# The MLP's down product as full 128x128 matmuls instead of 64x64 quarters, in a fused RWKV-7 and MLP kernel

## Chip, cores and metric

The kernel runs on one core of a Trainium2 chip. The metric is the device time of one execution in microseconds (us). Three runs of the kernel before took 823.68, 815.56 and 818.89 us; their median is 818.89. Besides, one execution was taken with the hardware profiler; every row of a profile is from that one execution.

TensorE (PE in the views) multiplies: a matmul holds a stationary operand, which a weight load (PEld) brings into the array, and streams the columns of the moving operand through it. VectorE is DVE, ScalarE ACT, GpSimd POOL, and SyncE SP; SP issues the DMA transfers here.

## The reference

An RWKV-7 recurrence over 768 steps for 4 batches and 8 heads of 40 channels, and then an MLP of 320 to 2048 to 320 features on its 3072 output rows, all in fp32:

```python
for t in range(S):                                   # attention, S = 768
    y[:, :, t] = np.einsum('bhd,bhde->bhe', rt, state)
    Sa = np.einsum('bhde,bhe->bhd', state, at)
    state_decay = state * wt[:, :, None, :] - np.einsum('bhd,bhe->bhde', Sa, bt)
    state = state_decay + np.einsum('bhd,bhe->bhde', vt, kt)
...
h = x @ w_in                                         # x: (3072, 320), w_in: (320, 2048)
g = h * (1.0 / (1.0 + np.exp(-1.702 * h)))
return (g @ w_out).astype(np.float32)                # w_out: (2048, 320)
```

The change concerns the last line, `g @ w_out`.

## The kernel before

**Work.** The sequence is cut into 12 chunks of 64 steps. A unit is one chunk of two batches, so there are 24 units, two for each chunk. For a unit the kernel prepares decays (`decay`, `prep`), solves the recurrence inside the chunk in a chain of small products (`solve`: a score N, then six `level` steps in two halves b, then the outputs y and the carried state z), and sends the result x through a DRAM tile into `xT`. After the second unit of a chunk the MLP of that chunk follows (`mlp`, L834), on 256 tokens: 4 batches of 64 steps.

**Products.** Every product in the file goes through the helper `mm` (L270), so all matmuls carry line 271. All of them are in 64x64 quarters of the array: `HALF` (L241) names the two halves of the 128 partitions and `QUARTERS` (L243) the order of the four combinations (half that is read, half that is written). In the down product (L851 to L862) a stationary tile is 64 rows of g (features) by 64 tokens, and the moving one is 64 rows of `w_out_sb` by 320 columns:

```python
for r, b in QUARTERS:
    o = p * 128 + b * 64
    mm(po[HALF[b], r, :DM], g[HALF[r], f % 2, o:o + 64], w_out_sb[HALF[r], f * DM:(f + 1) * DM], f == 0)
```

The two feature halves r of a block f of 128 features accumulate in different PSUM banks, bank r of a pair, and b names the token half on the partitions. So after 16 blocks f the result is the sum of two banks. Each fp32 product is executed as two passes, each with its own weight load: 1,536 calls of `mm` are 3,072 matmuls and 3,072 loads in the trace.

For one chunk, `up` (L837) makes the hidden layer in four tiles q of four blocks f; `gelu` (L846) brings each of them from PSUM into a buffer g (four buffers, `g=4` in L252). `down(p)` (L851) is called for each token half p (two batches). Its `part(m)` does two blocks f, 8 calls of `mm`, and there are eight parts for each p: 192 in all. One pair of banks serves one p. `store` (L867) then copies bank 0 into the buffer `ob` (ACT or DVE, L871), adds bank 1 to it on DVE (L873), and issues two output DMAs (L870). `ob` has one buffer.

**Order.** Nothing here is in program order. Each step is added to a planner (`Plan`, L59) as a task with a rank, the engines that may do it, an estimated cost on each, the data it reads and writes, and its PSUM pair (four pairs of two banks, `psum`, L265). `Plan.order` (L97) places tasks on the engines one after the other: of the tasks that are ready, the lowest rank goes first. Solving has ranks below 300, the MLP 10000 and more, so that ups and downs fill what the solver's chain leaves of TensorE. `paced` (L204) tries four release times for the MLP and keeps the plan that it finds shortest. For TensorE the planner also counts instructions (`instr`), since it assumes that they are fetched in blocks of 256 (`BLOCK`, `FETCH`, L65, and `fetched`, L133), and prefers tasks with fewer of them when it is ahead of the fetch. `pe` (L277) gives a TensorE task its cost: two passes of columns / 1.2 + 3 ns for each quartet, and 16 instructions. The instructions are then emitted in the order found; each engine works through its own in that order and waits on semaphores.

Of the kernel before, what the change touches and what calls it, by code (L numbers as in the profile page):

```python
# [49 lines left out]

class Task:
    def __init__(self, rank, engines, fn, pair, most, size):
        self.instr, self.sbuf = engines.pop("instr", 0), engines.pop("sbuf", False)
        self.rank, self.fn, self.pair, self.most, self.size = rank, fn, pair, most, size
        self.engines = engines
        self.after, self.then, self.release = set(), [], 0.0


class Plan:  # L59
# [5 lines left out]
    BLOCK, FETCH, BESIDE, AHEAD = 256, 3550.0, 0.4, 300.0  # L65
    DELAY = {"PE": 300.0, "DVE": 60.0, "ACT": 60.0, "POOL": 150.0, "SP": 800.0}

    LATENCY, RATE, SPREAD = 1200.0, 400.0, 1.3

    def __init__(self, slots, pairs):  # L70
        self.slots, self.pairs = slots, pairs
# [25 lines left out]
    def order(self):  # L97
# [10 lines left out]
        able, now, wire, out, many = [], 0.0, 0.0, [], set()  # L108
# [8 lines left out]
                return clear > len({o.pair[0] for o in able if o.most is not None and o.pair not in held and not any(k[0] == o.pair[0] for k in many)})  # L117
            return clear > 0 and sum(k[0] == t.pair[0] for k in many) < t.most

        issued, begun, shared = 0, 0.0, 0.0  # L120

        def fetch(at):
            took = self.FETCH
# [9 lines left out]
        def fetched(t, start):  # L133

            at, left, ns, block = start, t.instr, t.engines["PE"] / t.instr, begun
            room = self.BLOCK - issued % self.BLOCK
            while left >= room:
                at += room * ns
                left -= room
                at = block = max(at, block + fetch(block))  # L140
                room = self.BLOCK
            return at + left * ns, block
# [5 lines left out]
        while coming or able:  # L148
            while coming and coming[0][0] <= now:
                able.append(self.tasks[heapq.heappop(coming)[1]])  # L150
            able.sort(key=lambda t: (t.rank, t.n))
            took = None
            for e in free:
                if free[e] <= now:
                    took = next((t for t in able if e in t.engines and fits(t) and unread(t, e) <= now), None)
                    if took and e == "PE" and ahead(took) > self.AHEAD:

                        took = next((t for t in able if e in t.engines and fits(t) and ahead(t) < min(self.AHEAD, ahead(took))), took)
                    if took:
                        break  # L160
            if not took:
                later = [x for x in (*free.values(), *pairs, *(unread(t, e) for t in able for e in t.engines)) if now < x < float("inf")]
                now = min(later + ([coming[0][0]] if coming else []))
                continue
            t = took
            able.remove(t)
            t.engine = e
            end = now + t.engines[e]
            if e == "PE":
                end, begun = fetched(t, now)  # L170
                issued += t.instr
            if e == "POOL" or e == "DVE" and t.sbuf:

                shared = max(now, shared) + t.engines[e]
                end = max(end, shared)
            free[e] = end
            if e == "SP":
                wire = max(wire, end + self.LATENCY)
                running.append((wire, wire + self.SPREAD * t.size / self.RATE))
                end = wire = running[-1][1]  # L180
            if t.pair is not None:
                if e != "PE":
                    last.setdefault(t.pair, {})[e] = end
                if t.pair not in held:
                    held[t.pair] = next(i for i, p in enumerate(pairs) if p <= now)
                    pairs[held[t.pair]] = float("inf")
                    if t.most is not None:
                        many.add(t.pair)
                t.bank = held[t.pair]
                users[t.pair] -= 1  # L190
                if not users[t.pair]:
                    many.discard(t.pair)
                    pairs[t.bank] = end + self.DELAY[e]
            for o in t.then:
                o.ready = max(o.ready, end + (0.0 if o.engines.keys() == {e} else self.DELAY[e]))
                o.left -= 1
                if not o.left:
                    heapq.heappush(coming, (max(o.ready, o.release), o.n))
            t.start = now
            out.append(t)  # L200
# [24 lines left out]
def rwkv7_gelu_quick(ctx: ExitStack, tc: tile.TileContext, time_d, v_d, w_d, wc_d, ak_d, b_d, rv_d, w_in, w_out, out):  # L225
    nc = tc.nc
    H, D, S = 8, 40, out.shape[0] // 4
    DM = H * D
# [3 lines left out]
    PIECE = w_in.shape[2]  # L232
    NF = w_in.shape[0] * PIECE // DM
    NM = NF // 2
    NK = DM // 64
    NQ = NM // 2
# [4 lines left out]
    HALF = [slice(0, 64), slice(64, 128)]  # L241
    BITS = (0, 1)
    QUARTERS = [(0, 0), (1, 1), (0, 1), (1, 0)]  # L243
# [5 lines left out]
    banks = ctx.enter_context(tc.tile_pool(name="banks", bufs=1, space=bass.MemoryType.PSUM))  # L249

    plan = Plan(dict(logw=3, wc=3, G=1, wch=3, wz=2, time=2, ak=2, b=2, rv=2, FT=3, GT=1, kh=2, bh=2, bz=2,
                     A=1, Av=1, RV=2, W=2, W0=2, W1=2, E=2, E0=2, E1=2, edge=1, zraw=2, zT=1, saT=1, M=2, y=1, x=1, xT=3, g=4, ob=1), 4)  # L252
    tiles, psums, drams = {}, {}, {}

    def single(name, shape):
# [9 lines left out]
    def psum(t, name):  # L265
        if t.pair not in psums:
            psums[t.pair] = banks.tile([128, 2, 512], FP32, tag=f"pair{t.bank}", name=name)
        return psums[t.pair]

    def mm(o, lhsT, rhs, start):  # L270
        nc.tensor.matmul(o, lhsT, rhs, start=start, stop=True, skip_group_check=True)  # L271
# [5 lines left out]
    def pe(*sets):  # L277

        return {"PE": sum(n * 2 * max(58.0, cols / 1.2 + 3) for n, cols in sets), "instr": sum(16 * n for n, _ in sets)}

    def dve(n):
        return {"DVE": 170.0 + 1.03 * n}
# [4 lines left out]
    def any2(n):  # L287
        return {**act(n), **dve(n)}

    def copy(e):  # L290
        return nc.scalar.copy if e == "ACT" else nc.vector.tensor_copy
# [33 lines left out]
    edge = single("edge", [128, 2, 2, 2, 168])  # L325
# [508 lines left out]
    def mlp(c):  # L834
        R = 10000 + 100 * c

        def up(q, m, k):  # L837
            def go(t):
                ph, x = psum(t, "ps_up"), xT_of(c)[:, :, k]
                for r, h in QUARTERS:  # L840
                    mm(ph[HALF[h], r, m * 256:(m + 1) * 256], w_in_sb[HALF[r], 2 * q + m, k, h * 64:(h + 1) * 64], x[HALF[r]],
                       m == 0 and k == 0)
            plan.add(R + q, pe((1, 256)), go, reads=[("xs", (c, p)) for p in BITS] + [("weight", q)],
                     uses=[("xT", c)], room=[("g", c * NQ + q)], pair=("up", c * NQ + q), most=1)

        def gelu(q):  # L846
            plan.add(-45, act(1024), lambda t: nc.scalar.activation(  # L847
                g_of(c * NQ + q).rearrange("p m r n -> p r m n"), psum(t, "").rearrange("p r (m n) -> p r m n", m=2),
                ACT.Gelu_apprx_sigmoid), writes=[("g", c * NQ + q)], pair=("up", c * NQ + q))

        def down(p):  # L851
            serial = 2 * c + p

            def part(m):
                def go(t):
                    po, g = psum(t, "ps_down"), g_of(c * NQ + m // 2)[:, m % 2]
                    for f in (2 * m, 2 * m + 1):
                        for r, b in QUARTERS:
                            o = p * 128 + b * 64
                            mm(po[HALF[b], r, :DM], g[HALF[r], f % 2, o:o + 64], w_out_sb[HALF[r], f * DM:(f + 1) * DM], f == 0)  # L860
                parts = range(2 * m * DM // PIECE, (2 * (m + 1) * DM - 1) // PIECE + 1)
                plan.add(R + 10 * (p + 1) + m, pe((2, 320)), go, reads=[("g", c * NQ + m // 2)] + [("weight", NQ + n) for n in parts],  # L862
                         pair=("down", serial), most=1)
            for m in range(NM):
                part(m)

            def store(t):  # L867
                for b in BITS:
                    o = (2 * p + b) * S + c * C
                    nc.sync.dma_start(out[o:o + C, :], ob_of(serial)[HALF[b]])  # L870
            plan.add(-45, any2(320), lambda t: copy(t.engine)(ob_of(serial), psum(t, "")[:, 0, :DM]),  # L871
                     writes=[("ob", serial)], pair=("down", serial))
            plan.add(-45, dve(320), lambda t: nc.vector.tensor_add(ob_of(serial), ob_of(serial), psum(t, "")[:, 1, :DM]),  # L873
                     reads=[("ob", serial)], writes=[("out", serial)], pair=("down", serial))
            plan.add(-100, {"SP": 700.0}, store, reads=[("ob", serial), ("out", serial)], size=128 * DM * 4)

        for q in range(NQ):
            for m in BITS:
                for k in range(NK):
                    up(q, m, k)  # L880
            gelu(q)
        for p in BITS:
            down(p)

    for i in range(3):
        load_w(i)
# [105 lines left out]
```

## Time and profile before

| | |
|---|---|
| runs | 815.56, 818.89, 823.68 us |
| span of the profiled execution, first to last instruction | 816.7 us |
| mean granted TensorE clock | 0.994 of full |
| up product, matmuls | 3,840 of 64x256, 378 ns each |
| down product, weight loads | 3,072 of 64x64, 133 ns each |
| levels, matmuls with E | 5,888, 230 ns each on average over three shapes |
| DVE, final addition L873 | 24 of 128x320, 482 ns each |
| ACT or DVE, copy out of PSUM L871 | 19 on ACT (427 ns), 5 on DVE (492 ns) |
| ACT, gelu L847 | 48 of 128x1024, 1,026 ns each |
| ACT, copies of level results L726 | waited 176.7 us in 132 waits for the levels |
| output DMAs | 48 of 80 KB |

The page lists no separate time of the profiled execution beside its span; the span lies between the times of the runs. A matmul's length in the trace runs from its first read to a modelled end and so overlaps the next ones: quarters run beside each other, and lengths of single records don't add up to time. What a run of matmuls takes is read from start to start. "x16" behind a group is its number of records; in brackets stands how long the engine had been idle before, and what released it. "issue" is an idle time for which the profile shows no cause. The weight load has a row of its own (PEld).

### The profile page before, as it was taken

How to read it: one execution, taken by the hardware profiler on the slowest of the kernel's cores; microseconds unless marked ns; L12 is line 12 of the kernel's file. 1: busy time of each engine (PE TensorE's matmuls, PEld its weight loads, DVE VectorE, ACT ScalarE, POOL GpSimd, SP SyncE). 2: the span in 40 equal slices, each digit the busy share in tenths (PEclk: the TensorE clock that was granted, in tenths of full speed). 3: DMA queues.
4: the chain of work that ended last, by engine and by line, in shares of the span. 5: the costliest groups of instructions: out<-in, count | busy, mean ns of one | idle time of the engine just before them, and what ended most of it. 6: DMA issues, size and time to landing. Idle time of an engine off the chain costs nothing.

```text
span 816.7 us, 51357 instructions
## 1 busy us (share of the span) xinstructions
PE 749.6 (92%) x24192; PEld 636.1 (78%) x24192; DVE 477.7 (58%) x764; ACT 352.3 (43%) x603; POOL 153.3 (19%) x209
## 2 busy tenths in 40 slices
PE   4567887999999999999999989999999999999997
PEld 3556766787798888788888888887787887899785
DVE  7489778755755755756755654745556545455200
ACT  4376874444344253245254344355346345243210
POOL 4024052012202302302302302302103213200000
PEclk9899999999999999999999999999999999999999
DMA  9834452223403502412412512412403213110200
GB/s 348 329 110 146 136 194 72 70 69 89 134 17 91 152 20 86 133 45 82 138 45 68 152 44 74 141 46 72 142 15 98 71 50 92 40 33 4 60 10 18
DMA packets 32731, 76.31 MB, mean 93 GB/s; under 512 B 5096, under 2 KB 14312, under 8 KB 31496
## 3 DMA queue, kind: packets, MB, share of 16 engines
q1 hardware_dynamic: 32520, 73.03, 28.7%
q8 instruction: 190, 3.11, 1.6%
q14 instruction: 21, 0.17, 0.1%
HBM read 65.14 MB, written 7.86 MB: 89 GB/s over the span
## 4 chain that ended last, share of the span: by engine, by line
PE 79%; ACT 7%; DVE 6%; issue 4%; DMA 3%; SPq 1%; POOL 0%; ACTq 0%; DVEq 0%; POOLq 0%
PE ps_down L271 24%; PE ps_up L271 22%; PE ps_level L271 17%; PE ps_y L271 4%; PE ps_N L271 2%; ACT W L726 2%; PE ps_saT L271 1%; PE ps_Av L271 1%; PE ps_M L271 1%; PE ps_NT L271 1%; PE ps_A L271 1%; PE ps_RV L271 1%; PE ps_rz L271 1%; ACT L847 1%; PE ps_zT L271 1%
## 5 line engine op out<-in xcount | busy, mean ns | idle before, releaser
L271 PE MATMUL ps_up<-xT,w_sb 64*64 64x256 f32 x3840 | 274.5, 378 | 7.6 <-issue 4.5
L271 PE MATMUL ps_down<-w_sb,g 64*64 64x320 f32 x3072 | 243.8, 431 | 2.9 <-DVE w_sb L406 1.6
L726 ACT COPY W<-ps_level 128x672 f32<-128x672 f32 (+1 forms) x164 | 102.4, 626 | 184.2 <-PE ps_level L271 176.7
L271 PEld LDWEIGHTS ps_up<-xT,w_sb 64*64 64x64 f32 x3840 | 159.9, 134 | 27.3 <-issue 7.2
L271 PEld LDWEIGHTS ps_level<-W,E 64*64 64x64 f32 x5888 | 153.0, 134 | 27.9 <-issue 4.5
L271 PEld LDWEIGHTS ps_down<-w_sb,g 64*64 64x64 f32 x3072 | 130.9, 133 | 43.8 <-DVE w_sb L406 2.0
L271 PE MATMUL ps_level<-W,E 64*64 64x64 f32 (+2 forms) x5888 | 152.2, 230 | 7.8 <-issue 2.5
L721 DVE TENSOR_TENSOR E<-twice,ps_level 128x512 f32<-128x512 f32 x120 | 81.8, 686 | 87.8 <-ACT W L726 75.6
L538 POOL TENSOR_TENSOR kh<-time,G 128x320 f32<-128x320 f32 x23 | 20.8, 906 | 414.5 <-issue 289.3
L271 PE MATMUL ps_level<-W 64*64 64x64 f32 (+2 forms) x2560 | 69.4, 239 | 22.1 <-issue 10.3
L271 PEld LDWEIGHTS ps_level<-W 64*64 64x64 f32 x2560 | 66.2, 138 | 29.5 <-issue 15.0
L847 ACT ACTIVATE g<-ps_up 128x1024 f32<-128x1024 f32 x48 | 49.2, 1026 | 42.6 <-PE ps_up L271 42.2
L812 POOL TENSOR_TENSOR x<-y,FT 128x128 f32<-128x128 f32 x88 | 56.1, 667 | 0.7 <-DVE y L802 0.4
L705 DVE TENSOR_TENSOR W<-edge,ps_level 128x672 f32<-128x672 f32 x40 | 33.9, 850 | 12.2 <-PE ps_level L271 11.1
L530 POOL TENSOR_TENSOR ak<-ak,FT 128x512 f32<-128x512 f32 x20 | 27.9, 1394 | 64.1 <-DMA ak<-in_ak 55.8
L873 DVE TENSOR_TENSOR ob<-ob,ps_down 128x320 f32<-128x320 f32 x24 | 11.6, 482 | 48.0 <-ACT ob L871 45.7
L271 PE MATMUL ps_y<-RV,kh 64*64 64x104 f32 x768 | 37.1, 251 | 1.3 <-issue 1.3
L271 PE MATMUL ps_y<-M,bh 64*64 64x104 f32 x768 | 37.5, 250 | 0.5 <-issue 0.4
L726 DVE COPY W<-ps_level 128x672 f32<-128x672 f32 (+1 forms) x36 | 26.4, 733 | 14.2 <-PE ps_level L271 14.1
L271 PEld LDWEIGHTS ps_y<-RV,kh 64*64 64x64 f32 x768 | 29.0, 133 | 4.6 <-issue 2.9
L767 DVE TENSOR_TENSOR M<-ps_M,upper 128x512 f32<-128x512 f32 x24 | 16.6, 690 | 26.5 <-PE ps_M L271 26.4
L716 DVE TENSOR_TENSOR E<-twice,ps_level 128x256 f32<-128x256 f32 x40 | 16.8, 420 | 26.1 <-ACT W L726 16.9
(114 smaller groups left out, 986.0 us busy)
## 6 DMA issues: line engine op xcount, KB each, us to landing
time<-in_time SPq DMA_DIRECT2D x24, 480.0 KB
xT<-x_dram SPq DMA_DIRECT2D x48, 160.0 KB
ak<-in_ak SPq DMA_DIRECT2D x44, 160.0 KB
rv<-in_rv SPq DMA_DIRECT2D x44, 160.0 KB
wc<-in_wc SPq DMA_DIRECT2D x24, 264.0 KB
extra<-in_w_out SPq DMA_DIRECT2D x4, 1280.0 KB
logw<-in_w SPq DMA_DIRECT2D x24, 160.0 KB
RV<-in_v SPq DMA_DIRECT2D x24, 160.0 KB
```

The source lines that it names most:

```text
L271: nc.tensor.matmul(o, lhsT, rhs, start=start, stop=True, skip_group_check=True)
L530: plan.add(R, {"DVE": 690.0, "POOL": 1270.0, "sbuf": True}, lambda t: of(t.engine).tensor_mul(ahT(), ahT(), FT_of(i)), reads=T("ak", "FT") ...
L538: plan.add(R + 4, {"POOL": 870.0, "DVE": 490.0, "sbuf": True}, lambda t, n=n, dst=dst: of(t.engine).tensor_mul(dst(i)[:, :, :D], by_head(t ...
L705: plan.add(key, dve(672), lambda t: nc.vector.tensor_sub(W_of(s + 2)[:, :, b], edge[:, :, b], item(t)[:, :, :, :168]), reads=T("edge"), wr ...
L716: plan.add(key, dve(256), lambda t: nc.vector.tensor_tensor(E_of(es + 2)[:, :, b, :, 64:], wide(ident if early else twice).to_broadcast([1 ...
L721: plan.add(key, dve(512), lambda t: nc.vector.tensor_sub(E_of(es + 2)[:, :, b].rearrange("p h j (n t) -> p h (j n) t", n=2), wide(twice).t ...
L726: plan.add(key, any2(4 * (168 - lo)), lambda t: copy(t.engine)(W_of(s + 2)[:, :, b, :, lo:], item(t)[:, :, :, lo:168]), writes=keeps, pair ...
L767: plan.add(R + 4, dve(512), lambda t: nc.vector.tensor_tensor(M_of(i)[:, :, :64].rearrange("p (e j) t -> p e j t", e=2), psum(t, "")[:, :, ...
L812: of(t.engine).tensor_mul(x[:, b ^ u, b], y_of()[:, at], FT_of(i)[:, at])
L847: plan.add(-45, act(1024), lambda t: nc.scalar.activation(g_of(c * NQ + q).rearrange("p m r n -> p r m n"), psum(t, "").rearrange("p r (m ...
L873: plan.add(-45, dve(320), lambda t: nc.vector.tensor_add(ob_of(serial), ob_of(serial), psum(t, "")[:, 1, :DM]), reads=[("ob", serial)], wr ...
```

## The change

A down task now multiplies with the whole array. The stationary tile is 128 features by 128 tokens, the moving one 128 rows of `w_out_sb` by 320 columns, and one matmul does what a quartet did. The two token halves p of a chunk are done in the same task, each in a bank of its own of one PSUM pair. There are 8 tasks for a chunk, each of two blocks f and both p (4 calls of `mm`), 96 in all. No sum of banks is left: `store(p)` copies bank p into `ob` and issues the two output DMAs. `ob` gets two buffers. The planner's tasks get a mode, 64 or 128, and on TensorE it adds an assumed 200 ns (`SWITCH`) where the mode of a task differs from that of the one before it; the down tasks are the only ones with mode 128.

```diff
-        self.instr, self.sbuf = engines.pop("instr", 0), engines.pop("sbuf", False)
+        self.instr, self.sbuf, self.mode = engines.pop("instr", 0), engines.pop("sbuf", False), engines.pop("mode", 64)
...
-    LATENCY, RATE, SPREAD = 1200.0, 400.0, 1.3
+    LATENCY, RATE, SPREAD, SWITCH = 1200.0, 400.0, 1.3, 200.0
...
-        issued, begun, shared = 0, 0.0, 0.0
+        issued, begun, shared, mode = 0, 0.0, 0.0, 64
...
-                end, begun = fetched(t, now)
+                end, begun = fetched(t, now + (self.SWITCH if t.mode != mode else 0.0))
+                mode = t.mode
...
-                     A=1, Av=1, RV=2, W=2, W0=2, W1=2, E=2, E0=2, E1=2, edge=1, zraw=2, zT=1, saT=1, M=2, y=1, x=1, xT=3, g=4, ob=1), 4)
+                     A=1, Av=1, RV=2, W=2, W0=2, W1=2, E=2, E0=2, E1=2, edge=1, zraw=2, zT=1, saT=1, M=2, y=1, x=1, xT=3, g=4, ob=2), 4)
...
-        def down(p):
+        def down(m):
+            def go(t):
+                po, g = psum(t, "ps_down"), g_of(c * NQ + m // 2)[:, m % 2]
+                for f, p in product((2 * m, 2 * m + 1), BITS):
+                    mm(po[:, p, :DM], g[:, f % 2, p * 128:(p + 1) * 128], w_out_sb[:, f * DM:(f + 1) * DM], f == 0)
+            parts = range(2 * m * DM // PIECE, (2 * (m + 1) * DM - 1) // PIECE + 1)
+            plan.add(R + 10 + m, {"PE": 4 * 2 * (320 / 1.2 + 3), "instr": 16, "mode": 128}, go,
+                     reads=[("g", c * NQ + m // 2)] + [("weight", NQ + n) for n in parts], pair=("down", c), most=1)
+
+        def store(p):
             serial = 2 * c + p
 
-            def part(m):
-                def go(t):
-                    po, g = psum(t, "ps_down"), g_of(c * NQ + m // 2)[:, m % 2]
-                    for f in (2 * m, 2 * m + 1):
-                        for r, b in QUARTERS:
-                            o = p * 128 + b * 64
-                            mm(po[HALF[b], r, :DM], g[HALF[r], f % 2, o:o + 64], w_out_sb[HALF[r], f * DM:(f + 1) * DM], f == 0)
-                parts = range(2 * m * DM // PIECE, (2 * (m + 1) * DM - 1) // PIECE + 1)
-                plan.add(R + 10 * (p + 1) + m, pe((2, 320)), go, reads=[("g", c * NQ + m // 2)] + [("weight", NQ + n) for n in parts],
-                         pair=("down", serial), most=1)
-            for m in range(NM):
-                part(m)
-
-            def store(t):
+            def go(t):
                 for b in BITS:
                     o = (2 * p + b) * S + c * C
                     nc.sync.dma_start(out[o:o + C, :], ob_of(serial)[HALF[b]])
-            plan.add(-45, any2(320), lambda t: copy(t.engine)(ob_of(serial), psum(t, "")[:, 0, :DM]),
-                     writes=[("ob", serial)], pair=("down", serial))
-            plan.add(-45, dve(320), lambda t: nc.vector.tensor_add(ob_of(serial), ob_of(serial), psum(t, "")[:, 1, :DM]),
-                     reads=[("ob", serial)], writes=[("out", serial)], pair=("down", serial))
-            plan.add(-100, {"SP": 700.0}, store, reads=[("ob", serial), ("out", serial)], size=128 * DM * 4)
+            plan.add(-45, any2(320), lambda t: copy(t.engine)(ob_of(serial), psum(t, "")[:, p, :DM]),
+                     writes=[("ob", serial)], pair=("down", c))
+            plan.add(-100, {"SP": 700.0}, go, reads=[("ob", serial)], size=128 * DM * 4)
...
-        for p in BITS:
-            down(p)
+        for m in range(NM):
+            down(m)
+        for p in BITS:
+            store(p)
```

Since the planner orders all tasks anew with these costs, the order of instructions on every engine differs between the two kernels, also outside the MLP.

## The prediction

> **What bounds the kernel now.** I read the page first, then the stretches of 80 us, then the timeline around the down product and at the end, then the waits of TensorE. The page:
>
> ```profile
> span 816.7 us, 51357 instructions
> PE 749.6 (92%) x24192; PEld 636.1 (78%) x24192; DVE 477.7 (58%) x764; ACT 352.3 (43%) x603; POOL 153.3 (19%) x209
> ...
> q8 instruction: 190, 3.11, 1.6%
> ...
> PE 79%; ACT 7%; DVE 6%; issue 4%; DMA 3%; SPq 1%; POOL 0%; ACTq 0%; DVEq 0%; POOLq 0%
> ...
> L271 PE MATMUL ps_down<-w_sb,g 64*64 64x320 f32 x3072 | 243.8, 431 | 2.9 <-DVE w_sb L406 1.6
> ```
>
> TensorE carries 79% of the chain that ended last. 24,192 matmuls and as many weight loads are 48,384 instructions, 189 blocks of 256; queue 8 shows 190 fetches of 16 KB, so the instruction stream itself comes in by DMA. By stretches (us, then busy time and count for each engine):
>
> ```profile
> 240.00:320.00 80.00, 78.40 (x2530) 69.53 (x2526) 47.65 (x83) 33.94 (x59) 17.54 (x25) 1.00 0.28 81
> 780.00:817.00 37.00, 32.14 (x535) 23.86 (x524) 0.97 (x2) 4.96 (x6) 0.00 (x0) 0.99 0.06 15
> ```
>
> From 160 us on TensorE is busy 94 to 98% of every stretch while DVE, the next, has 60%. But busy is not streaming, so I look at start times. Timeline, TensorE alone (start, length, group):
>
> ```profile
> 434.77 1.31 PE L271 MATMUL ps_down<-w_sb,g 64*64 64x320 f32 x16
> 435.85 0.41 PE L271 MATMUL ps_y<-RV,kh 64*64 64x104 f32 x8
> ...
> 437.28 1.31 PE L271 MATMUL ps_down<-w_sb,g 64*64 64x320 f32 x16
> 438.35 0.64 PE L271 MATMUL ps_level<-W,E 64*64 64x40 f32 x29
> ```
>
> A part of the down product (16 records: two f, four quarters, two passes of each fp32 product) gives way to the next task after 1.08 us, and nothing is lost at the border: the next task starts while the last pass is still in flight (length 0.43 us). All of it is 64*64. At the end:
>
> ```profile
> 796.64 14.93 PEld L271 LDWEIGHTS ps_down<-w_sb,g 64*64 64x64 f32 x224
> 796.86 15.28 PE L271 MATMUL ps_down<-w_sb,g 64*64 64x320 f32 x224
> ```
>
> 224 records are 56 passes of four quarters; 15.28 less the 0.16 us by which the last one outlives its streaming (below) is 15.12, or 0.270 us a pass: 0.833 ns a column. Fresh weights for every quarter and pass cost nothing there.
>
> **What the Trainium skill says.** (1) "TensorEngine Tiling (Array Packing)", Key Properties: "Changing tiling mode (not just tile) drains the TensorE". It gives no price, and before has one mode only, so its trace cannot confirm it. This decides the forecast. (2) "TensorE: Matmul & The Clock Gate", LDWEIGHTS: a load takes its columns / 1.2 ns, so 53 ns for 64 and 107 for 128; and Measured speedup vs the span model: a load overlaps running matmuls only in another row group. The 56 passes above contradict the second: each quarter loads while its own matmul streams. (3) "Runtime: NRT & Kernel Launch", Instruction fetch mechanics: blocks of 16 KiB, 256 instructions, fetched while the present one runs, the cost "mostly hidden". The block size agrees; "mostly" has exceptions here, such as this stop inside one task that waits for nothing:
>
> ```profile
> 134.49 0.34 PE L271 MATMUL ps_y<-RV,kh 64*64 64x104 f32 x3
> 135.86 0.31 PE L271 MATMUL ps_y<-RV,kh 64*64 64x104 f32 x3 [1.03 <-issue]
> ```
>
> **The change, part by part**, against the profiled execution's span of 816.7 us; the median of the runs, 818.9, is 2.2 above it, and I carry that 2.2 over.
>
> *Streaming.* Before: 192 parts x 4 passes of a quartet x 0.270 = 207 us. After: 12 chunks x 8 m x 4 full matmuls x 2 passes = 768 passes of the same 320 columns, x 0.270 = 207 us. A quartet uses the whole array already, so nothing is won. No row shows a 128-column load or matmul; bounds for this term: 0 (loads hidden, as now) to 768 x 0.107 = +82 us (no load hidden). I take 0.
>
> *Instructions.* 3,072 matmuls and 3,072 loads become 768 and 768: 4,608 fewer, 18 blocks of 189. That pays only where a block runs faster than it can be fetched. In 100 to 780 us TensorE's waits for "issue" add up to 9.2 us by its matmuls and 22.7 by its loads (the first understates, since the modelled ends cover a gap's start). Counting gaps between starts over 100 ns beyond the streaming time, about 15 us stand at one fixed place in the 256-instruction block. Most are in stretches of up products and levels, which the change doesn't thin out. Cutting the built order of both programs into blocks of 256 and giving each matmul its streaming time (0.833 ns a column, at least 58 ns a quartet), blocks beyond the 19th fall short of 3.7 us, near the mean fetch interval of the trace, by 25.7 us in all before and 15.5 after: 40% less. 40% of 15 us is **-6 us**; bounds -2 and -15. The first 19 blocks (about 80 us) hold no down product and stay.
>
> *Mode switches.* In the changed program's order on TensorE the down product stands in 88 groups (two of them of more than one part), which makes 175 borders between 64 and 128 wide. Price of one: a matmul's record outlasts its streaming by 429 - 267 = 162 ns (320 columns) and 221 - 53 = 168 (64), so an empty pipeline costs about 0.165 us; if the next weights are read only then, the 53 or 107 ns of a load come on top, 0.245 on average; with that load's fixed part too (133 - 53 = 80 ns) 0.325. Bounds 0 to 0.325. I take the middle of 0.165 and 0.245, 0.205: 175 x 0.205 = **+36 us**. TensorE is busy 96% of 100 to 780 us, so there's almost no idle time to hide it.
>
> *Final sum and copies.* 24 DVE additions of 0.48 us go (11.6 us). DVE has 40% free and only the last one is on the path (812.65). Now two ACT copies follow each other there (0.43 each against 0.43 + 0.49), and behind the last matmul stand four output DMAs where two stood, at 0.56 us each to issue (median in the view by tile): the second store's first waits for the first store's two: **+0.6 us**. Earlier ones are covered by the next chunk's matmuls; ob gets a second buffer for it.
>
> *Longer parts.* A part holds TensorE 2.16 us instead of 1.08 (plus the switches), and level matmuls queued behind it come later, then the ACT copy and DVE update that wait for them. ACT's copies already idle 176.7 us for the levels and TensorE loses nothing by that, because ups and downs fill in: 0, bound +10. g is read by both halves at once, so it frees earlier: 0, TensorE being the bound.
>
> *Order elsewhere.* The planner orders every engine anew. SP issues the same transfers in number, in another order, the two halves' outputs now one after the other; DVE takes over five multiplications from POOL (0.84 to 0.93 us each in the rows of L535 and L530 on DVE, hidden by its free 40%), and ACT loads its function table 47 times instead of 43: 4 x 1.28 us on an engine that is 43% busy. 0, bound +5 where a gelu waits behind such a load and TensorE has no other task.
>
> Sum: 816.7 + 36 - 6 + 0.6 = 847.3 in the profile; with 2.2, **849 us** as median.
>
> **Rivals.** (A) The above, chance 0.55, own range 831 to 871 (0.1 to 0.325 us a switch). (B) The other side: modes change without a drain, since quarters and full matmuls are the same array and the seam is as smooth as between two 64*64 tasks at 435.85. Then only the fetch is left: 818.9 - 6 + 0.6 = 813.5; with all 15 us of fetch stalls gone 804.5. It decides below 5.4 / 175 = 0.03 us a switch (below 0.08 with the full 15). For it: no seam shows anything today; against it: the skill's sentence. Chance 0.22. (C) A short drain, 0.03 to 0.1 us: 819 to 831, mid 823; chance 0.14. (D) The 128-column load isn't hidden: +82 us on top of A, 931. Against it: quarters hide theirs. Chance 0.05. (E) The chain of levels becomes the bound through the longer parts: 88 visits x 0.5 us later on average = +44 on top of C, 867. Against it: the engines behind TensorE idle for it. Chance 0.04.
>
> **Numbers.** About 1% is what a measurement of this kernel can tell from no change (810.7 to 827.1). Faster: most of B's lower half, 0.16. Same: the rest of B and most of C, 0.18. Slower: A, D, E and C's end, 0.66. Range 806 to 876: below it about 0.07 of B, above it D, part of E and A's tail, some 0.12.
>
> **What would show it.** Right: ps_down 128 wide x768 at 0.27 us a pass inside a run (the last 24 matmuls, 48 passes, in 13 us); a gap of about 0.2 us in starts at each border of ps_down; TensorE's total instructions 4,608 fewer; blocks fetched 172. Wrong: borders without a gap (B); passes of 0.37 us or more (D); DVE or ACT first in the chain with TensorE idle before levels (E); or fetch stalls gone altogether.

## The result and the profile after

Four runs of the changed kernel took 841.38 to 846.0 us, median 843.1; four runs of the kernel before on the same chip had a median of 819.41. The ratio is **1.0267, 95% interval 1.0204 to 1.0329**: slower. The medians lie 24 us apart, and 843.1 is 6 us below the 849 that were forecast. (The ratio is the one on record for undisturbed executions; the quotient of the medians is 1.029.) The profiled execution took 842.63 us with a span of 840.8 and a mean clock of 0.987 (before: span 816.7, clock 0.994). The page of the changed kernel:

```profile
span 840.8 us, 46706 instructions
PE 781.1 (93%) x21888; PEld 630.5 (75%) x21888; DVE 472.5 (56%) x748; ACT 354.0 (42%) x607; POOL 143.6 (17%) x201
...
q8 instruction: 172, 2.82, 1.4%
...
PE 79%; ACT 5%; DVE 3%; issue 2%; DMA 1%; SPq 0%; POOL 0%; ACTq 0%; DVEq 0%
...
L272 PE MATMUL ps_down<-w_sb,g 128*128 128x320 f32 x768 | 230.2, 444 | 0.4 <-DVE W L727 0.4
```

The counts are those of the forecast: 2,304 matmuls and 2,304 loads fewer, 172 fetches of instructions instead of 190. TensorE still carries 79% of the chain. The trap in this page is the busy time: TensorE is 31.5 us busier while it streams the same columns, because a matmul's record outlasts its streaming (by 0.165 us, as the prediction works out) and so covers much of a pause. A drain looks like work here. A stretch in the middle of the work shows the same (us, then busy time and count for PE, PEld, DVE, ACT, POOL):

```profile
240.00:320.00 80.00, 77.27 (x2328) 62.03 (x2324) 43.74 (x77) 32.77 (x57) 12.54 (x18) 1.00 0.25 72
```

TensorE is almost as busy as before (77.3 of 80 us against 78.4), but the matmuls that start in this stretch stream for 72.6 us instead of 75.4 (counted as below). The counts of 2,328 and 2,530 can't be set against each other, since one full matmul stands for four. The cause is seen only from start to start. The timeline of TensorE's matmuls in the changed kernel (start, length, group), two visits to the down product with a level between them:

```profile
457.58 2.42 PE L272 MATMUL ps_down<-w_sb,g 128*128 128x320 f32 x8
459.93 0.68 PE L272 MATMUL ps_level<-W,E 64*64 64x40 f32 x32
460.54 1.88 PE L272 MATMUL ps_down<-w_sb,g 128*128 128x320 f32 x6
```

and the weight loads of the same stretch:

```profile
457.58 1.91 PEld L272 LDWEIGHTS ps_down<-w_sb,g 128*128 128x128 f32 x8
459.93 0.56 PEld L272 LDWEIGHTS ps_level<-W,E 64*64 64x64 f32 x32 [0.44 <-issue]
460.54 1.64 PEld L272 LDWEIGHTS ps_down<-w_sb,g 128*128 128x128 f32 x7
```

From the start of one down part to the next are 2.96 us. Eight passes stream in 8 x 0.270 = 2.16 and eight quartets of 40 columns in 8 x 0.058 = 0.46, so 0.34 us are lost in one visit: two borders. The loads stop for 0.44 us at the border with "issue" as the reason: the next weights aren't read ahead over the border, as they are inside a run of one shape. Inside a run of full matmuls nothing is lost, as the end of the changed kernel shows:

```profile
822.13 13.19 PE L272 MATMUL ps_down<-w_sb,g 128*128 128x320 f32 x48
...
835.40 0.75 ACT L868 COPY ob<-ps_down 128x320 f32<-128x320 f32 x2 [12.05 <-PE ps_down L272]
```

13.19 less a tail of 0.165 are 13.0 us for 48 passes, 0.271 each: the 128-column loads are hidden there. Behind it stand the two ACT copies.

**Where the time went.** I counted, over all starts of TensorE after 100 us, what passes between matmuls beyond their streaming (0.833 ns a column and 3 ns, at least 58 ns a quartet); I call it the loss. "Seams" is the loss at the borders of a visit (the 88 groups of down product), 0.354 us being the median of one. "At fetches" is what falls on the one place in the block of 256 instructions where TensorE's stops pile up. "At half clock" is what is lost in stretches after 100 us in which the granted clock was half of full. Each column is one profiled execution.

| us | before | after | after's order in quarters (first experiment) |
|---|---|---|---|
| seams | 0 | 88 x 0.354 = 31.2 | 0 |
| rest of the loss, all | 50.0 | 41.4 | 59.6 |
| of it at fetches | 15.5 | 10.2 | 20.8 |
| of it at half clock | 0 | 1.4 | 6.7 |

With 0.9 us more before 100 us and 0.9 more behind the last matmul (5.0 to 5.9), 31.2 - 8.6 + 1.8 = 24.4, the growth of the span (24.1) within 0.3 us.

The last row is a cost of its own. In these traces the granted clock changes on a grid of 3.41 us, and from 100 us to the last matmul it is either full or half. Cut along that grid, the 14 traces of this case have 2,975 stretches at full clock, and after 36 of them one at half clock follows. In each of the 36 the matmuls that start there fill at most 37% of the stretch by their streaming time (the highest is 0.3729), in all 2,939 others they fill more (the lowest is 0.3734). So a pause of some 2.1 us that falls into one stretch is followed by another in which 1.7 us more can be lost (estimates: 63% and half of 3.41 us).

### The profile page after: what moved, and what is told of

It reads as the page before. It is cut to its first block, busy times and chain, and to the rows that moved or that the text cites. A ratio compares the mean times of both kernels' runs of the same rounds, so it can differ in the third digit from the quotient of the medians.

```text
span 840.8 us, 46706 instructions
## 1 busy us (share of the span) xinstructions
PE 781.1 (93%) x21888; PEld 630.5 (75%) x21888; DVE 472.5 (56%) x748; ACT 354.0 (42%) x607; POOL 143.6 (17%) x201
## 4 chain that ended last, share of the span: by engine, by line
PE 79%; ACT 5%; DVE 3%; issue 2%; DMA 1%; SPq 0%; POOL 0%; ACTq 0%; DVEq 0%
PE ps_down L272 25%; PE ps_up L272 22%; PE ps_level L272 16%; PE ps_y L272 4%; PE ps_N L272 2%; PE ps_saT L272 1%; PE ps_M L272 1%; PE ps_rz L272 1%; PE ps_RV L272 1%; PE ps_Av L272 1%; PE ps_A L272 1%; PE ps_zT L272 1%; PE ps_NT L272 1%; ACT L848 1%; ACT W L727 1%
## 5 line engine op out<-in xcount | busy, mean ns | idle before, releaser
L272 PE MATMUL ps_down<-w_sb,g 128*128 128x320 f32 x768 | 230.2, 444 | 0.4 <-DVE W L727 0.4
L272 PEld LDWEIGHTS ps_down<-w_sb,g 128*128 128x128 f32 x768 | 138.7, 189 | 57.2 <-issue 4.3
L272 PEld LDWEIGHTS ps_up<-xT,w_sb 64*64 64x64 f32 x3840 | 153.2, 134 | 34.9 <-issue 11.1
L727 ACT COPY W<-ps_level 128x672 f32<-128x672 f32 (+1 forms) x157 | 98.4, 629 | 179.6 <-PE ps_level L272 171.9
L272 PEld LDWEIGHTS ps_level<-W,E 64*64 64x64 f32 x5888 | 146.5, 134 | 32.1 <-issue 13.4
L272 PE MATMUL ps_level<-W 64*64 64x104 f32 (+2 forms) x2560 | 69.9, 246 | 18.8 <-issue 9.8
L706 DVE TENSOR_TENSOR W<-edge,ps_level 128x672 f32<-128x672 f32 x40 | 33.9, 850 | 21.8 <-PE ps_level L272 19.7
L575 ACT COPY Av<-ps_Av 128x320 f32<-128x320 f32 x23 | 9.8, 425 | 76.6 <-PE ps_Av L272 76.6
L727 DVE COPY W<-ps_level 128x416 f32<-128x416 f32 (+1 forms) x43 | 30.7, 714 | 11.2 <-PE ps_level L272 11.2
L717 DVE TENSOR_TENSOR E<-twice,ps_level 128x256 f32<-128x256 f32 x40 | 16.6, 416 | 26.9 <-ACT W L727 19.5
L793 DVE TENSOR_TENSOR zraw<-ps_y,bz 128x320 f32<-128x320 f32 x20 | 9.8, 490 | 37.2 <-PE ps_y L272 37.2
L868 ACT COPY ob<-ps_down 128x320 f32<-128x320 f32 x22 | 8.3, 429 | 52.4 <-PE ps_down L272 52.4
```

The costliest lines, as they stand in the source:

```text
L575: plan.add(R + 1, any2(320), lambda t: copy(t.engine)(Av_of(i).rearrange("p e b n -> p b e n"), psum(t, "")[:, :, :160].rearrange("p b (e ...
L706: plan.add(key, dve(672), lambda t: nc.vector.tensor_sub(W_of(s + 2)[:, :, b], edge[:, :, b], item(t)[:, :, :, :168]), reads=T("edge"), wr ...
L717: plan.add(key, dve(256), lambda t: nc.vector.tensor_tensor(E_of(es + 2)[:, :, b, :, 64:], wide(ident if early else twice).to_broadcast([1 ...
L727: plan.add(key, any2(4 * (168 - lo)), lambda t: copy(t.engine)(W_of(s + 2)[:, :, b, :, lo:], item(t)[:, :, :, lo:168]), writes=keeps, pair ...
L793: nc.vector.tensor_add(new, got, bz_of(i)[:, :, 64:].rearrange("p (u j) d -> p u j d", u=2))
```

## Experiments

The theory is that of the prediction: TensorE empties at each change between 64 and 128 wide, some 0.2 us a border. Its main rivals are that longer parts on an engine that works in order delay what waits behind them, and that the new plan is simply a worse one. The ratios are to the kernel before on the same chip; its medians were 822.6 us for the first four experiments (by their order on record), 819.07 for the next four and 814.57 for the last four. They are those on record, which differ from the quotients of the medians by up to 0.5%. "Loss" is counted as above, in one profiled execution of each kernel.

**The new order in quarters.** One part undone: the tasks, the plan and the order of after, but each full matmul is a quartet again.

```diff
-                    mm(po[:, p, :DM], g[:, f % 2, p * 128:(p + 1) * 128], w_out_sb[:, f * DM:(f + 1) * DM], f == 0)
+                    for r, b in QUARTERS:
+                        o = p * 128 + b * 64
+                        mm(po[HALF[b], r, :DM], g[HALF[r], f % 2, o:o + 64], w_out_sb[HALF[r], f * DM:(f + 1) * DM], f == 0 and p == 0)
```

> The order of instructions of the changed kernel, but each full matmul is four 64x64 quarters again (both token halves are added into the same sums, so the output is another; the streaming is the same). Seams theory (each visit of the 128-wide mode costs about 0.32 us, 88 visits): no seam is left, so 819 us, between 815 and 824, with fetch stalls back at about 15 us. Rival, the new order with parts of 2.16 us costs the time and not the mode: 838 to 846, as the changed kernel. Rival, a full matmul streams slower than a quartet: 819 too, told apart by the next run.

833.38 us, 1.0157 [1.0096, 1.0218]: between the two, and neither foresaw it. Without one change of mode the new order alone costs some 12 us of span (829.1 against 816.7), 9.6 of them as loss after 100 us. Going from here to after adds 31.2 us of seams and yet only about 10 us of time: the rest of the loss falls from 59.6 to 41.4. The 9.6 are not only late levels: 5.3 of them stand at fetches and 6.7 in four stretches at half clock, of which the kernel before has none after 100 us, while the other waits fell.

**Full matmuls in the old order.** The other part alone: one token half at a time as before, each quartet as one full matmul, a DVE copy where the sum was.

```diff
-                        for r, b in QUARTERS:
-                            o = p * 128 + b * 64
-                            mm(po[HALF[b], r, :DM], g[HALF[r], f % 2, o:o + 64], w_out_sb[HALF[r], f * DM:(f + 1) * DM], f == 0)
+                        mm(po[:, 0, :DM], g[:, f % 2, p * 128:(p + 1) * 128], w_out_sb[:, f * DM:(f + 1) * DM], f == 0)
```

> The order of instructions of the kernel before, with full 128x128 matmuls in it, one token half to a part (the second bank is not used, and the DVE addition is a copy of the same size). 147 groups of down, 293 borders, the same 768 passes. Seams theory: 819 + 147 x 0.32 - 5 (fewer fetches) = 861, between 855 and 868. Rival, order: 814 to 820. Rival, slower wide passes: 843, as the changed kernel, since the number of passes is the same.

856.09 us, 1.0405 [1.0368, 1.0442], as the seams say. The timeline of TensorE in this kernel:

```profile
387.67 1.34 PE L271 MATMUL ps_down<-w_sb,g 128*128 128x320 f32 x4
388.94 0.41 PE L271 MATMUL ps_y<-RV,kh 64*64 64x104 f32 x8
```

A part that gave way after 1.08 us in the kernel before (434.77 to 435.85) now does so after 1.27; the other share of the 0.355 us a visit (median) stands ahead of its start and in the first narrow load after it. 147 visits x 0.355 = 52.2 us of seams, but the rest of the loss fell from 50.0 to 31.2, so 33.4 us remain. At fetches it fell by only 2.2 (15.5 to 13.3); most of the 19 us that vanished are other waits. That data and instructions arrive during the pauses is how I read it; it is argued, not shown. Set beside after, this run shows the price of the new order with full matmuls: the rest of the loss is 31.2 us in the old order and 41.4 in the new one, 10.2 more, as it was 9.6 more in quarters.

**Parts of twice and of four times the length.** Fewer visits, if seams were all: the tasks of after with 4 or 8 blocks f instead of 2 (48 and 24 tasks). Core of the edit for four times:

```diff
-                for f, p in product((2 * m, 2 * m + 1), BITS):
+                for f, p in product(range(8 * m, 8 * (m + 1)), BITS):
...
-        for m in range(NM):
+        for m in range(NM // 4):
```

> The changed kernel with 48 down tasks of twice the length (4.3 us), 47 groups, 93 borders. Seams theory: 819 + 47 x 0.32 - 5 + 0.6 = 830, between 825 and 834. Rival, order and longer parts: 843 or more, since levels wait longer behind a part. Slower wide passes: 843.

> The changed kernel with 24 down tasks of four times the length (8.6 us), 24 groups, 47 borders. Seams theory: 819 + 24 x 0.32 - 5 + 0.6 = 822, between 817 and 828 if TensorE is not left without ready work between the parts. Rival, order and longer parts: 850 or more. If seams fall and levels come late at once, it lies between, 828 to 845, with DVE or ACT ahead of TensorE in the chain.

869.22 us, 1.0569 [1.0525, 1.0614], and 898.39 us, 1.0919 [1.0878, 1.0961]. The seams theory missed both by 35 to 80 us, on the wrong side. The seams did what it says (0.357 and 0.352 us a visit, so 16.8 and 8.4 us in all), but the rest of the loss rose to 83.5 and 117 us. TensorE in the kernel with four times the length:

```profile
411.14 8.88 PE L272 MATMUL ps_down<-w_sb,g 128*128 128x320 f32 x32
419.95 0.68 PE L272 MATMUL ps_level<-W,E 64*64 64x40 f32 x32
```

For 8.8 us the levels stand behind one part. TensorE's waits in this kernel between 100 and 900 us (waiting group, what it waited for: total us, times, longest):

```profile
PE ps_up L272 <- DMA xT<-x_dram: 16.6, 11, 5.2
PE ps_level L272 <- issue: 10.0, 12, 2.1
PE ps_level L272 <- ACT g L848: 5.4, 7, 1.5
```

The chain of levels now ends late, so x comes late, and the ups have nothing to multiply: 16.6 us of waiting for `xT` against 4.2 in after. Waits for "issue" have grown more, to 28.5 us in all from 4.9, and the loss at fetches is some 39 us against 10. Idle TensorE has a further price, seen in the view of the cores:

```profile
core 0: 893.9 us, clock 0.965
```

0.035 x 893.9 = 31 us of clock not granted, against 0.006 x 816.7 = 5 in the kernel before. The drops do follow the waits: each of them after 100 us begins behind a stretch of 3.41 us that TensorE filled by 37% or less, as in all traces here. 26.6 us were lost at half clock after 100 us, against 1.4 in after. So of the 76 us by which the rest of the loss exceeds that of after, about two thirds stand at fetches and at half clock, and the smaller part is other waits.

**Half-sized tiles.** Is it the full array that costs, or another shape too? The old order with tiles of 64 rows by 128 columns, and with 128 rows by 64 columns:

```diff
-                        for r, b in QUARTERS:
-                            o = p * 128 + b * 64
-                            mm(po[HALF[b], r, :DM], g[HALF[r], f % 2, o:o + 64], w_out_sb[HALF[r], f * DM:(f + 1) * DM], f == 0)
+                        for r in BITS:
+                            mm(po[:, r, :DM], g[HALF[r], f % 2, p * 128:(p + 1) * 128], w_out_sb[HALF[r], f * DM:(f + 1) * DM], f == 0)
```

> Order of the kernel before; each quartet is two matmuls of 64 rows by 128 columns (one for each feature half, in two banks as before, and the sum stays). 147 groups, 293 borders, 3,072 instructions fewer. Any change of the tile's shape costs a seam, and a 128-column load is exposed as with full matmuls: as the full matmuls in that order, ratio to before 1.035 to 1.045. Rival, only the full array drains, half-array tiles do not: ratio 0.985 to 1.000, by the fetches saved, with no pause at the borders.

```diff
-                        for r, b in QUARTERS:
+                        for b in BITS:
                             o = p * 128 + b * 64
-                            mm(po[HALF[b], r, :DM], g[HALF[r], f % 2, o:o + 64], w_out_sb[HALF[r], f * DM:(f + 1) * DM], f == 0)
+                            mm(po[HALF[b], 0, :DM], g[:, f % 2, o:o + 64], w_out_sb[:, f * DM:(f + 1) * DM], f == 0)
```

> Order of the kernel before; each quartet is two matmuls of 128 rows by 64 columns (one for each 64 tokens, both in one bank, no sum; the DVE addition is a copy of the same size). 147 groups, 293 borders. Any change of the tile's shape costs, but the load exposed on the way in is of 64 columns (53 ns less by the trace's loads and the skill's price): ratio to before 1.028 to 1.038, 0.30 us a visit instead of 0.355. Rival, only the full array drains: 0.985 to 1.000.

855.45 us, 1.0425 [1.0364, 1.0485], and 849.44 us, 1.0368 [1.0303, 1.0433]. Both pay. The timelines of TensorE, first of 64 rows by 128 columns:

```profile
381.76 1.35 PE L271 MATMUL ps_down<-w_sb,g 64*128 64x320 f32 x8
383.04 0.41 PE L271 MATMUL ps_y<-RV,kh 64*64 64x104 f32 x8
```

then of 128 rows by 64 columns:

```profile
381.83 1.30 PE L271 MATMUL ps_down<-w_sb,g 128*64 128x320 f32 x8
383.06 0.41 PE L271 MATMUL ps_y<-RV,kh 64*64 64x104 f32 x8
```

1.28 and 1.23 us instead of 1.08. A visit costs 0.359 us in the first and 0.309 in the second; the 0.05 between them is the load: the first pass after the border takes 0.373 us with 128 columns to load and 0.320 with 64, where one inside a run takes 0.269. So a load of 104 or 51 ns stands open at the border. The Trainium skill's "TensorE: Matmul & The Clock Gate", LDWEIGHTS, gives columns / 1.2, 107 and 53 ns: it agrees.

**Seams doubled.** After with the second of the four matmuls of each part done as a quartet, so that each part goes from wide to quarters and back once more. Nothing else moves.

```diff
-                    mm(po[:, p, :DM], g[:, f % 2, p * 128:(p + 1) * 128], w_out_sb[:, f * DM:(f + 1) * DM], f == 0)
+                    if f % 2 or p == 0:
+                        mm(po[:, p, :DM], g[:, f % 2, p * 128:(p + 1) * 128], w_out_sb[:, f * DM:(f + 1) * DM], f == 0)
+                    else:
+                        for r, b in QUARTERS:
...
```

> The changed kernel and its order, but the second of the four matmuls of each part is done as four quarters (the sums of one token half are wrong by that), so each part has two stretches of 128 instead of one: 184 visits instead of 88, the same passes. Seams theory: 96 x 0.355 = 34 us more than the changed kernel if nothing absorbs a seam, about 25 if the same share is absorbed as so far (the net price was 0.23 to 0.28 us a visit): ratio to before 1.055 to 1.072. Rival, the time is in the order or in the passes: as the changed kernel, 1.027 plus at most 0.005.

876.85 us, 1.0681 [1.0622, 1.0741]. The difference to after is (1.0681 - 1.0267) x 819 = 33.9 us for 96 more visits, 0.353 us each: the price by the clock on the wall, apart from any plan (the two intervals leave about 7 us either way, so 0.28 to 0.43). The weight loads of one part:

```profile
470.64 0.30 PEld L272 LDWEIGHTS ps_down<-w_sb,g 128*128 128x128 f32 x2
471.38 0.21 PEld L272 LDWEIGHTS ps_down<-w_sb,g 64*64 64x64 f32 x8 [0.44 <-issue]
472.08 0.84 PEld L272 LDWEIGHTS ps_down<-w_sb,g 128*128 128x128 f32 x4 [0.49 <-issue]
473.35 0.56 PEld L272 LDWEIGHTS ps_level<-W,E 64*64 64x64 f32 x32 [0.44 <-issue]
```

Three borders, three stops. The part takes 2.71 us where it took 2.35. The rest of the loss stayed at 42.0 us (after: 41.4), so on balance nothing was absorbed of these, though 7.0 us of it are now lost at half clock (after: 1.4). Why these pauses replaced no waits, and those of the old order did, isn't shown.

**What makes the new order cost.** Four kernels, the first three without wide tiles. Replanned: the tasks of after in quarters, with the planner told so (64 instructions, no mode). Short: one block f a task, both token halves, 1.08 us. Old long: the kernel before with four blocks f for one token half, 2.16 us. Wide and short: after with one block f a task.

```diff
-            plan.add(R + 10 + m, {"PE": 4 * 2 * (320 / 1.2 + 3), "instr": 16, "mode": 128}, go,
+            plan.add(R + 10 + m, {"PE": 4 * 2 * (320 / 1.2 + 3), "instr": 64, "mode": 64}, go,
```

> Both token halves in one task, in quarters, and planned as such (64 instructions, no mode): the tasks of the changed kernel without its mode (both halves are added into the same sums, so the output is another). If parts of 2.16 us cost nothing by themselves: ratio to before 0.995 to 1.005. If the longer parts cost: 1.01 to 1.02, as the quarters in the changed kernel's order did (1.016).

```diff
-            plan.add(R + 10 + m, {"PE": 4 * 2 * (320 / 1.2 + 3), "instr": 16, "mode": 128}, go,
+            plan.add(R + 10 + m, {"PE": 2 * 2 * (320 / 1.2 + 3), "instr": 32, "mode": 64}, go,
...
-        for m in range(NM):
+        for m in range(NF):
```

> Both token halves in one task, in quarters and planned as such, but one block f to a task: 192 tasks of 1.08 us, the old length (both halves are added into the same sums, so the output is another). If the length of a part is what cost 3.6% in the run with parts of 2.16 us: ratio to before 0.995 to 1.01. If it is the two halves in one task, or the luck of a plan: 1.02 or more.

```diff
-                    for f in (2 * m, 2 * m + 1):
+                    for f in range(4 * m, 4 * m + 4):
...
-            for m in range(NM):
+            for m in range(NQ):
```

> The kernel before, token half after token half, with four blocks f to a part instead of two: parts of 2.16 us, quarters, nothing else changed. Length theory: ratio to before 1.02 to 1.04, with TensorE waiting before levels and DVE or ACT behind it. If length costs nothing: 0.995 to 1.005.

```diff
-            plan.add(R + 10 + m, {"PE": 4 * 2 * (320 / 1.2 + 3), "instr": 16, "mode": 128}, go,
+            plan.add(R + 10 + m, {"PE": 2 * 2 * (320 / 1.2 + 3), "instr": 8, "mode": 128}, go,
...
-        for m in range(NM):
+        for m in range(NF):
```

> The changed kernel with one block f to a task: 192 full-array tasks of 1.08 us, 143 visits. Seams theory with the same absorption as in the old order with full matmuls (52 us of seams, 18 absorbed): ratio to before 1.035 to 1.045. If short parts give back what the longer ones cost and absorb no less: 1.025 to 1.035. Below 1.0 in no theory.

| kernel | us | ratio, 95% |
|---|---|---|
| replanned, quarters, 2.16 us, both halves | 849.38 | 1.0356 [1.0269, 1.0442] |
| short, quarters, 1.08 us, both halves | 818.67 | 1.0046 [1.0019, 1.0073] |
| old long, quarters, 2.16 us, one half | 833.38 | 1.0191 [1.0162, 1.022] |
| wide and short, 1.08 us and seams | 834.67 | 1.0216 [1.0181, 1.0251] |

Both halves in a task at 1.08 us cost 0.5%; 2.16 us cost 1.9 to 3.6% with one half or both, without any seam. That speaks for the length of the part, though each length was tried in few plans. The sizes were not foreseen: replanned came above the 1.01 to 1.02 that its expectation gives for a cost of length, old long just under its 1.02 to 1.04. TensorE's waits in the kernel before with long parts, between 100 and 830 us:

```profile
PE ps_level L271 <- DVE E L707: 4.6, 3, 3.2
PE ps_up L271 <- DMA xT<-x_dram: 3.3, 4, 1.3
```

They are the waits of the long parts above on a small scale: levels that come late, then `xT` (1.6 us before, 3.3 here). But most of what this kernel loses beyond the kernel before is lost at half clock, behind waits of TensorE of which this is the clearest. Its timeline:

```profile
706.18 0.44 PE L271 MATMUL ps_level<-W,E 64*64 64x40 f32 x16 [3.16 <-ACT G L501]
706.44 1.85 PE L271 MATMUL ps_up<-xT,w_sb 64*64 64x256 f32 x16
...
710.08 1.07 PE L271 MATMUL ps_up<-xT,w_sb 64*64 64x256 f32 x16
```

and the stretch behind the wait (the 0.50 is the granted clock):

```profile
706.60:710.00 3.40, 3.40 (x72) 2.46 (x67) 0.65 (x2) 0.43 (x1) 0.00 (x0) 0.50 0.02 5
```

Sixteen up matmuls of one shape take 1.85 us at half clock and 1.07 at full. Five such stretches after 100 us hold 9.0 of the 12 us by which the loss (62.0) exceeds that of the kernel before, which has none; in replanned it is 12.9 of 26 us. So a good part of what these two kernels lose is clock: TensorE runs dry for long enough that it falls. Wide and short fell below what both theories gave it: 143 visits x 0.355 = 50.8 us of seams, but only 14.0 us of other loss. Its interval and that of after overlap, so I can't say that short parts are better for full matmuls.

**Another plan.** The kernel before with the planner's window changed; the tasks are the same, in another order.

```diff
-    ROUNDS, WINDOW, SHARE = 4, 5000.0, 1.0
+    ROUNDS, WINDOW, SHARE = 4, 4800.0, 1.0
```

> The kernel before with one constant of the planner moved by 4% (the window by which MLP tasks are released ahead), so that the same tasks come out in another order. It shows what the luck of a plan is worth: ratio to before 0.99 to 1.01 if the order alone moves the time little; beyond 1.02, differences of a few per cent between two plans mean little.

809.26 us, **0.989 [0.9853, 0.9927]** (0.993 by the medians), the fastest version of all, with nothing changed but the luck of the order: the loss is 38.0 us instead of 50.0. So 1% of any comparison that plans anew may be luck, and perhaps more, since this is one other plan. This limits how finely the length effect is known (1.9% and 3.6% for two kernels with parts of the same length), and leaves the seams alone, since 0.354 us is read inside a trace and confirmed where the order didn't move.

## Why the prediction was right, and which step failed

The likeliest case happened (rival A's mechanism at a somewhat lower price), the size was 849 against 843. Term by term, forecast and found, in us:

| step | forecast | found |
|---|---|---|
| mode borders | +36 (175 x 0.205) | +31.2 (88 visits x 0.354, 0.177 a border) |
| longer parts, order elsewhere | 0 (bounds +10 and +5) | +9.6, after's order in quarters against before (5.3 at fetches, 6.7 at half clock, others less) |
| fewer fetches | -6 (-2 to -15) | -10.6 at the fetches, -5.3 at half clock, -2.3 at other waits, against that order |
| start, end and copies | +0.6 | +1.8 |
| sum | +30.6 | +24.4 |

*Streaming*, 0 (bound +82): right, 0.271 us a pass with fresh 128-column weights. The doubt in the prediction about the Trainium skill's sentence that a load overlaps only in another row group ("TensorE: Matmul & The Clock Gate", Part 3, The mechanism; the prediction names the heading after it) is settled for this case: a load for all rows runs under a matmul on all rows. The same section also names a background weight buffer as a second way, which the prediction passed over; the runs fit it and don't show it.

*Mode switches*: the mechanism was right and the price 16% high (0.205 against 0.177), with two errors that partly offset one another, which is luck. Of a visit's 0.354 us, about 0.090 pass before the first wide matmul, 0.104 are its load, 0.094 pass behind the last one, and 0.05 to 0.065 are the first narrow load. So the drain is about 0.09 us and not the 0.165 us by which a record outlasts its streaming: the modelled end of a record is no measure of when the array is free. And the load lies open in full at both borders, about 0.08 us on average, where I had put 0.04. The sentence of the Trainium skill's "TensorEngine Tiling (Array Packing)", Key Properties, that a change of mode drains TensorE agrees with these pauses, and now has a price here.

*Longer parts*: this step failed. "TensorE loses nothing by that, because ups and downs fill in: 0" overlooked that the filler is the one that is long, and that a TensorE that runs dry loses clock as well. While a down part runs, a level that has become ready can't start; and ups fill in only while there is an `xT`, which comes out of that same chain. With quarters alone the ratio goes from 1.005 at 1.08 us a part to 1.019 and 1.036 at 2.16; with full matmuls from 1.027 at 2.16 to 1.057 at 4.3 and 1.092 at 8.6. The bounds of +10 and +5 together held. The 9.6 in quarters and the 10.2 with full matmuls agree, but how much of them is length and how much is luck of the plan isn't separated: another plan of the same tasks moved the time by 1.1%, which is as much.

*Fewer fetches*: -5.3 against before looks like the forecast's -6, but is a sum of two things, so its nearness is in part luck. The new order in quarters has 5.3 more at fetches than before, and the full matmuls take 10.6 away. (The prediction's 3.7 us isn't the mean interval of the fetches: between 100 and 780 us that is 4.1, the median 3.9.) The 7.6 us that vanish elsewhere with the seams were no step of the prediction at all: "there's almost no idle time to hide it" was wrong. 50 us of loss stood in the kernel before, and a pause that comes first can take the place of a wait that would have come. 5.3 of the 7.6 were lost at half clock, in four such stretches where after has one; how the other 2.3 divide between data and engines stays open.

*Rivals*: B and C (no or a short drain) ended below 0.1 us a border and are out at 0.177 (C's middle is 825 and not 823, which changes nothing); D (loads not hidden) is out, except for the first pass of a visit; E (levels become the bound through longer parts) names an effect that is there, in after at most some 10 us on top of A, and that outweighs the seams only from 4.3 us a part on.

## What to carry to other kernels

A tile shape that differs from its neighbours' on TensorE cost a fixed price for each visit here, 0.31 to 0.36 us; it pays only where a visit is long or saves more than that, and the array gave nothing for it, since the quarters already filled it (0.270 us a pass against 0.271). But don't gather visits into long ones on an engine that also serves a dependent chain without measuring: length cost as well here, and at twice and four times the length more than the borders it saved. Look at the granted clock behind long waits before blaming the waits alone. Before believing a gain or loss of 1% from an edit that makes a planner start anew, plan the old work once more in another way and see how far that moves the time.

## What was not expected of the hardware

All three shapes that were tried beside 64x64 pay, not the full array alone: 0.354 us there and back for 128x128, 0.359 for 64x128, 0.309 for 128x64. Within one shape fresh weights of 128 columns cost nothing for 48 passes on end, and the first load after a border costs its whole length (104 ns for 128 columns, 51 for 64), so the reading ahead of weights stops at the border. After 100 us the clock fell to half behind every full-clock stretch of 3.41 us that TensorE's streaming filled by 37% or less, 36 times in 14 traces, and behind no other. And short waits of TensorE aren't simply additive: 52 us of pauses put into the old order made the profiled span only 38 us longer (855.0 against 816.7), of which fewer fetches explain about 2.
